# Preparing the first pair's queries in two pieces, and the second pair later, in an attention and MoE kernel

## The chip, the cores and the metric

The kernel runs on one core of a Trainium2 chip. Its engines are TensorE (PE), VectorE (DVE), ScalarE (ACT), GpSimd (POOL) and SyncE (SP, which here only requests transfers). The metric is the device time of one launch in microseconds (us).

## What is computed

Attention with rotary embedding over 2 x 8 heads of 576 positions and 64 columns, and behind it two MLPs on the 1152 tokens. Cut to what matters:

```python
q_rot, k_rot = (rotate(q), rotate(k))
scores = scale * np.matmul(q_rot, k_rot.transpose(0, 1, 3, 2))
scores = scores - np.max(scores, axis=-1, keepdims=True)
attn = np.exp(scores)
attn = attn / (np.sum(attn, axis=-1, keepdims=True) + 1e-09)
x = np.matmul(attn, v)             # heads side by side: 1152 x 512
h = np.maximum(x @ w_in, 0.0)      # d_ff 2048
x = h * h @ w_out
out = ((x @ w_a) * (x @ w_b)) @ w2_out   # d_ff 1536
```

## The kernel before

The heads are taken in eight pairs. Of a pair, one tile `X` (128 partitions, the two heads above each other) holds queries and keys, each a second time with the halves swapped, so that rotation is a product with the cosines and sines in `cs` and a sum into `rot`. f32 numbers are split into a high part (a cast to the f32r type) and a low part (the rest). For every pair a tile `SK` holds queries, keys and the low part of the keys for both heads, with the high part of the queries in one half of the partitions and their low part in the other, so that a matmul with the keys in both halves sums them.

`first_pair` (L160) makes pair 0 and writes `SK[0]` directly. `prepare` (L151) makes the other pairs: for keys (`qi` 1) and queries (`qi` 0) a product over 1152 columns (L154) and a sum (L155) on the engine given in `engs`, a cast to the high part on ScalarE (L156), the low part on POOL (L157). `place` then copies high and low parts into `SK` by four DMAs on SP's queue (L142). There is one buffer `rot` and one pair of buffers `hi`, `lo` for all pairs, and `SK` has two buffers.

The work of a pair is nine blocks. For block i, `emit_S` makes the scores (four matmuls of 288 columns; the ninth block, for both heads' last 64 queries, ten), `emit_max` their maximum on VectorE (L214), `emit_exp` the exponentials with their sums on ScalarE (L220), and `emit_T` (three blocks later) the transposes on PE, copied from PSUM by ScalarE or VectorE (`evac`). Scores have two PSUM buffers, so block i+2 waits for the exponentials of block i. The products with V (`av_units`) of a pair lie between the blocks of the next; `emit_scale` spreads the reciprocals of the sums over partitions by small bf16 matmuls with `sel` and `ident16`, and these need a copy named `rows`. Behind the last pair come the MLPs (`unit1`, `out1`, `unit2`, `out2`), whose weights are fetched into `raw` tiles and prepared by `prep_weight`, four of them while the attention still runs.

The order on each engine is not the order in which the code is written: a scheduler lays the instructions of all engines out by its own estimates, and each engine then runs its list strictly in order (PE may load weights ahead). Pools with few buffers decide what has to wait. `X` of pair 0 and of pair 2 share a buffer, so the load of pair 2 waits for the last step that reads the queries of pair 0.

Of the kernel before, what the change touches and what calls it, by code (L numbers as in the profile page):

```python
# [7 lines left out]
F32 = mybir.dt.float32  # L8
F32R = mybir.dt.float32r
BF16 = mybir.dt.bfloat16  # L10
I32 = mybir.dt.int32
I64 = mybir.dt.int64
AF = mybir.ActivationFunctionType
ALU = mybir.AluOpType
AX = mybir.AxisListType

P = 128
S = 576
# [9 lines left out]
DM = 512  # L28
# [5 lines left out]
def attention_moe_moe2_kernel(ctx: ExitStack, tc: tile.TileContext, qk, rope, vm, vt, ident_in, sel_in, w_in, w_out, w_a, w_b, w2_out, out):  # L34
    nc = tc.nc
    act, dve, pool, pe = nc.scalar, nc.vector, nc.gpsimd, nc.tensor

    const = ctx.enter_context(tc.tile_pool(name="const", bufs=1))
# [5 lines left out]
    wpools = [ctx.enter_context(tc.tile_pool(name="wa", bufs=NWA))]  # L44

    ident = const.tile([P, P], F32, name="ident")
    ident16 = const.tile([P, P], BF16, name="ident16")
    sel = const.tile([18, 6, P], BF16, name="sel")
    X = {1: xpool.tile([P, 2, 2, S], F32, tag="x", name="X1")}
    xb = [xpool.tile([P, 2, KC, TB], F32R, tag="x", name=f"x{n}") for n in range(NTB)]  # L50

# [49 lines left out]
    LOFF = (1280, 1344)  # L101
    MAIN = (0, 128)

    def half(h):
        return slice(64 * h, 64 * h + 64)
# [51 lines left out]
            pool.tensor_tensor(out=lo[qi], in0=rot[:, qi, :], in1=hi[qi].bitcast(F32), op=ALU.subtract)  # L157
        place(p)

    def first_pair():  # L160
        sk, x = SK[0], X[0]

        def own(qi, h):
            off = (QOFF, KOFF)[qi][h]
            return sk[half(h), h, off:off + S]

        def cross(qi, h):
            off = (QOFF, KOFF)[qi][h]
            return sk[half(1 - h), h, off:off + S]

        for qi in (1, 0):
            for n in range(2):
                dve.tensor_tensor(out=x[:, n, qi, :], in0=x[:, n, qi, :], in1=cs[:, n, :], op=ALU.mult)
            dve.tensor_tensor(out=rot[:, qi, :], in0=x[:, 0, qi, :], in1=x[:, 1, qi, :], op=ALU.add)
            if qi:
                for h in range(2):
                    act.copy(own(1, h), rot[half(h), 1, :])
                    if h == 0:
                        act.copy(cross(1, h), rot[half(h), 1, :])
                    pool.tensor_tensor(out=sk[half(h), h, LOFF[h]:LOFF[h] + S], in0=rot[half(h), 1, :], in1=own(1, h).bitcast(F32), op=ALU.subtract)  # L180
        for h in range(2):
            act.copy(own(0, h), rot[half(h), 0, :])
            dve.tensor_tensor(out=cross(0, h), in0=rot[half(h), 0, :], in1=own(0, h).bitcast(F32), op=ALU.subtract)  # L183
            if h == 0:
                dve.tensor_copy(cross(1, 1), rot[half(1), 1, :])

    SP, PT, PTT, PR, ST = {}, {}, {}, {}, {}

# [147 lines left out]
    NB = 9 * NPAIR  # L336

    load_qk(0)
    load_qk(1)
    nc.sync.dma_start(out=ident, in_=ident_in)  # L340
    sel32 = g2.tile([18, 6, P], F32, tag="r", name="sel32")
    nc.sync.dma_start(out=sel32, in_=sel_in)
    zero_fills(0)
    zero_fills(1)
    first_pair()
    prepare(1, (dve, dve))
    emit_S(0)
    avq = []
    for i in range(NB + LT):
        p, j = divmod(i, 9)  # L350
        if i == 4:
            dve.tensor_copy(ident16, ident)
            dve.tensor_copy(sel, sel32)
        if i + 1 < NB:
            emit_S(i + 1)
        if i < NB:
            emit_max(i)
            emit_exp(i)
        if 0 <= i - LT:
            emit_T(i - LT)  # L360
        if p > 0:
            if j == LT + 1 and p <= NPAIR:
                avq += av_units(p - 1)
            for _ in range(2 if j > LT else 1):
                if avq:
                    avq.pop(0)()
        if j == 5 and i < NB:
            load_v(p)
        if p + 1 < NPAIR:
            n = p + 1  # L370
            if j == 0 and p > 0:
                load_qk(n)
            if j == 1 and p > 0:
                prepare(n, (dve, pool))
    while avq:
        avq.pop(0)()
# [198 lines left out]
```

## Time and profile before

| | us |
|---|---|
| median of three timed runs (613.55 to 614.51) | 613.93 |
| profiled execution | 613.54 |
| its span, first to last instruction | 611.8 |
| PE busy | 584.6 (96%) |
| VectorE, ScalarE, POOL busy | 333.6, 321.4, 257.2 |

The busy time of PE is near the whole span, and the granted clock is full (9 of 9 tenths, or 1.00) in every slice. The page's 40 slices of 15.3 us show PE at 0 tenths in the first, at 6 in the second and at 9 from the third on, except for the last. So what a change of the start is worth is read there, and from how far PE has come in its fixed list at a given time.

### The profile page before, as it was taken

Reading aid. Unit: us, or ns where it says so; the run is one execution under the profiler, and the core shown is the slowest. Engines: PE = TensorE matmul, PEld = TensorE weight load, DVE = VectorE, ACT = ScalarE, POOL = GpSimd, SP = SyncE. Lnnn points to the kernel's source line nnn. Section 1 sums busy time; section 2 is a strip of 40 time slices with the busy share of each in tenths; the row PEclk is TensorE's granted clock in tenths of the full one; section 3 lists DMA queues with packets and bytes.
Section 4 is the critical chain, followed back from the end, with each engine's and each line's share of the span. In section 5 each row is a group of like instructions: output and inputs, shape, how many; then the busy total and the mean of one; then the engine's idle time right before and its main releaser. Section 6 shows DMA issues by size and latency. Waiting matters only on the chain.

```text
span 611.8 us, 8929 instructions
## 1 busy us (share of the span) xinstructions
PE 584.6 (96%) x3368; PEld 520.3 (85%) x3368; DVE 333.6 (55%) x550; ACT 321.4 (53%) x685; POOL 257.2 (42%) x278
## 2 busy tenths in 40 slices
PE   0699999999999999999999999999999999999997
PEld 0567665666759999999999999999988999889986
DVE  5987578865525665676764467664440653221122
ACT  3477777786747776873671455554543653102200
POOL 4567655652115853770670433544421444202110
PEclk9999999999999999999999999999999999999999
DMA  6675756544001444433331213323220440000012
GB/s 230 183 191 149 210 169 182 135 130 109 20 2 70 138 138 138 138 132 110 121 121 35 83 55 104 108 99 118 90 69 7 142 128 1 0 1 2 0 53 103
DMA packets 20678, 61.41 MB, mean 100 GB/s; under 512 B 3337, under 2 KB 3721, under 8 KB 19739
## 3 DMA queue, kind: packets, MB, share of 16 engines
q1 hardware_dynamic: 20635, 60.85, 32.6%
q8 instruction: 26, 0.43, 0.3%
q14 instruction: 17, 0.14, 0.1%
HBM read 48.16 MB, written 2.36 MB: 83 GB/s over the span
## 4 chain that ended last, share of the span: by engine, by line
PE 92%; DVE 5%; DMA 1%; issue 1%; ACT 1%; SPq 0%; DVEq 0%; ACTq 0%
PE av L317 8%; PE s L205 7%; PE h L391 5%; PE y L391 5%; PE h L393 5%; PE h L392 5%; PE y L393 5%; PE y L392 5%; PE t L275 5%; PE a L391 4%; PE a L393 4%; PE b L391 4%; PE b L393 4%; PE a L392 4%; PE b L392 4%; PE o L467 4%
## 5 line engine op out<-in xcount | busy, mean ns | idle before, releaser
L411 POOL TENSOR_TENSOR g<-v,g 128x384 fp32r<-128x384 f32 x84 | 85.2, 1016 | 132.9 <-ACT g L410 132.9
L205 PE MATMUL s<-sk 128*128 128x288 f32 x336 | 64.9, 322 | 20.3 <-DVE sk L183 15.0
L205 PEld LDWEIGHTS s<-sk 128*128 128x128 f32 x336 | 48.6, 195 | 39.1 <-DVE sk L183 15.0
L410 ACT CAST g<-v 128x384 fp32r<-128x384 f32 x84 | 42.9, 511 | 62.2 <-DVE v L409 62.1
L214 DVE TENSOR_REDUCE st<-s 128x1 f32<-128x576 f32 x72 | 53.7, 751 | 31.2 <-PE s L205 31.1
L391 PE MATMUL h<-x,w_i 128*128 128x384 f32 x192 | 64.2, 335 | 0.0
L392 PE MATMUL h<-x,w_i 128*128 128x384 f32 x192 | 64.1, 334 | 0.0
L393 PE MATMUL h<-x,w_i 128*128 128x384 f32 x192 | 64.1, 334 | 0.0
L391 PE MATMUL y<-g,w_o 128*128 128x384 f32 x192 | 64.1, 334 | 0.0
L392 PE MATMUL y<-g,w_o 128*128 128x384 f32 x192 | 64.1, 334 | 0.0
L393 PE MATMUL y<-g,w_o 128*128 128x384 f32 x192 | 64.1, 334 | 0.0
L220 ACT ACTIVATE P<-s,st 128x576 f32<-128x576 f32 x72 | 53.6, 745 | 13.2 <-DVE st L214 13.0
L317 PE MATMUL av<-PT,V 128*64 128x384 f32 (+1 forms) x256 | 52.4, 425 | 0.0
L275 PE MATMUL t<-ident,P 128*128 128x128 f32 x288 | 45.9, 280 | 2.4 <-DVE PT L260 2.2
L393 PE MATMUL a<-yb,w_a 128*128 128x384 f32 x144 | 48.1, 334 | 0.0
L391 PE MATMUL a<-yb,w_a 128*128 128x384 f32 x144 | 48.1, 334 | 0.0
L392 PE MATMUL a<-yb,w_a 128*128 128x384 f32 x144 | 48.1, 334 | 0.0
L391 PE MATMUL b<-yb,w_b 128*128 128x384 f32 x144 | 48.1, 334 | 0.0
L392 PE MATMUL b<-yb,w_b 128*128 128x384 f32 x144 | 48.1, 334 | 0.0
L393 PE MATMUL b<-yb,w_b 128*128 128x384 f32 x144 | 48.1, 334 | 0.0
L409 DVE TENSOR_TENSOR v<-b,s 128x384 f32<-128x384 f32 x36 | 19.9, 554 | 50.8 <-PE b L393 50.8
L467 PE MATMUL o<-w,g 128*128 128x512 f32 (+1 forms) x112 | 42.8, 382 | 0.0
(118 smaller groups left out, 1337.8 us busy)
## 6 DMA issues: line engine op xcount, KB each, us to landing
raw_i<-in_w_in SPq DMA_DIRECT2D x16, 512.0 KB, 3.4
raw_o<-in_w_out SPq DMA_DIRECT2D x16, 512.0 KB, 3.2
X<-in_qk SPq DMA_DIRECT2D x7, 1152.0 KB, 5.4
raw_a<-in_w_a SPq DMA_DIRECT2D x12, 512.0 KB, 3.3
raw_b<-in_w_b SPq DMA_DIRECT2D x12, 512.0 KB, 3.3
raw<-in_w_out SPq DMA_DIRECT2D x12, 512.0 KB, 3.4
sk<-hi_lo SPq DMA_DIRECT2D x14, 432.0 KB, 5.1
sk<-hi_lo SPq DMA_DIRECT2D x14, 288.0 KB, 5.7
```

The lines of the kernel that those rows point to most:

```text
L205: pe.matmul(s[:, b, c:c + n], lhs, rhs, start=(m < 2), stop=(m >= len(mm) - len(cuts)), skip_group_check=(j == 8))
L214: dve.tensor_reduce(out=ST[p][:, 0, j:j + 1], in_=SP[i][:, :, 0:288], op=ALU.max, axis=AX.XY, negate=True)
L220: act.activation(pr[:, h, :].rearrange("p (b n) -> p b n", b=2), SP.pop(i)[:, :, 0:288], AF.Exp, bias=st[:, 0, j:j + 1], scale=1.0, accum_ ...
L275: pe.transpose(t[:, k * P:(k + 1) * P], flat[:, c0:c0 + P], ident)
L317: pe.matmul(AVT[p, r][half(h), 0:n], V[p][:, h, k, :], PT[p][:, h, k, q0:q0 + n], start=False, stop=(k == 3), skip_group_check=True)
L391: pe.matmul(dst, wh, mh, start=first, stop=False)
L392: pe.matmul(dst, wh, ml, start=False, stop=False)
L393: pe.matmul(dst, wl, mh, start=False, stop=last)
L409: dve.tensor_tensor(out=val, in0=src, in1=other, op=ALU.mult)
L410: act.copy(gt[:, 0, c], val)
L411: pool.tensor_tensor(out=gt[:, 1, c], in0=val, in1=gt[:, 0, c].bitcast(F32), op=ALU.subtract)
L467: pe.matmul(dst, gt[:, 1, c], w[:, 0, d], start=False, stop=(k == G - 1))
```

## The change

- `load_qk(1)` is taken out of the start. Pair 1's `X` is now requested on ScalarE's queue, from within `first_pair`, after the first cross copy of the keys.
- `first_pair` takes a range of columns and is called twice: for all keys and queries 0 to 191, and for queries 192 to 575 (named `c`). All casts and copies into `SK[0]` are on ScalarE and all subtractions on VectorE; POOL no longer takes part. `emit_S(0)`, `emit_S(1)`, `emit_max(0)`, `emit_exp(0)` stand between the two calls, and `emit_max(1)` within the second.
- From the first of these calls until the loop's block 3 a manual order holds on PE, ScalarE, VectorE and POOL: the written one.
- `prepare(1)` moves from the start into the loop (block 2) and has its queries on POOL instead of VectorE, as the later pairs.
- `ident16` and `sel` are no longer bf16 tiles that VectorE fills by casts, but views of the f32 tiles: the upper half of each word, every second bf16 element.
- Two memsets of `raw` tiles at block 3 keep the first weight fetches from being requested before.

```diff
--- before.py
+++ after.py
@@ -44,8 +44,9 @@
     wpools = [ctx.enter_context(tc.tile_pool(name="wa", bufs=NWA))]
 
     ident = const.tile([P, P], F32, name="ident")
-    ident16 = const.tile([P, P], BF16, name="ident16")
-    sel = const.tile([18, 6, P], BF16, name="sel")
+    sel32 = const.tile([18, 6, P], F32, name="sel")
+    ident16 = ident.bitcast(BF16).rearrange("p (n two) -> p n two", two=2)[:, :, 1]
+    sel = sel32.bitcast(BF16).rearrange("p k (n two) -> p k n two", two=2)[:, :, :, 1]
     X = {1: xpool.tile([P, 2, 2, S], F32, tag="x", name="X1")}
     xb = [xpool.tile([P, 2, KC, TB], F32R, tag="x", name=f"x{n}") for n in range(NTB)]
 
@@ -157,7 +158,7 @@
             pool.tensor_tensor(out=lo[qi], in0=rot[:, qi, :], in1=hi[qi].bitcast(F32), op=ALU.subtract)
         place(p)
 
-    def first_pair():
+    def first_pair(c0, c1):
         sk, x = SK[0], X[0]
 
         def own(qi, h):
@@ -168,21 +169,28 @@
             off = (QOFF, KOFF)[qi][h]
             return sk[half(1 - h), h, off:off + S]
 
-        for qi in (1, 0):
+        def rotated(qi, c):
             for n in range(2):
-                dve.tensor_tensor(out=x[:, n, qi, :], in0=x[:, n, qi, :], in1=cs[:, n, :], op=ALU.mult)
-            dve.tensor_tensor(out=rot[:, qi, :], in0=x[:, 0, qi, :], in1=x[:, 1, qi, :], op=ALU.add)
-            if qi:
-                for h in range(2):
-                    act.copy(own(1, h), rot[half(h), 1, :])
-                    if h == 0:
-                        act.copy(cross(1, h), rot[half(h), 1, :])
-                    pool.tensor_tensor(out=sk[half(h), h, LOFF[h]:LOFF[h] + S], in0=rot[half(h), 1, :], in1=own(1, h).bitcast(F32), op=ALU.subtract)
+                dve.tensor_tensor(out=x[:, n, qi, c], in0=x[:, n, qi, c], in1=cs[:, n, c], op=ALU.mult)
+            dve.tensor_tensor(out=rot[:, qi, c], in0=x[:, 0, qi, c], in1=x[:, 1, qi, c], op=ALU.add)
+
+        c = slice(c0, c1)
+        if c0 == 0:
+            rotated(1, slice(0, S))
+            act.copy(own(1, 0), rot[half(0), 1, :])
+        rotated(0, c)
+        if c0:
+            emit_max(1)
         for h in range(2):
-            act.copy(own(0, h), rot[half(h), 0, :])
-            dve.tensor_tensor(out=cross(0, h), in0=rot[half(h), 0, :], in1=own(0, h).bitcast(F32), op=ALU.subtract)
-            if h == 0:
-                dve.tensor_copy(cross(1, 1), rot[half(1), 1, :])
+            if c0 == 0 and h == 1:
+                act.copy(own(1, 1), rot[half(1), 1, :])
+            act.copy(own(0, h)[:, c], rot[half(h), 0, c])
+            if c0 == 0:
+                act.copy(cross(1, h), rot[half(h), 1, :])
+                dve.tensor_tensor(out=sk[half(h), h, LOFF[h]:LOFF[h] + S], in0=rot[half(h), 1, :], in1=own(1, h).bitcast(F32), op=ALU.subtract)
+            dve.tensor_tensor(out=cross(0, h)[:, c], in0=rot[half(h), 0, c], in1=own(0, h)[:, c].bitcast(F32), op=ALU.subtract)
+            if c0 == 0 and h == 0:
+                act.dma_start(out=X[1], in_=qk[1])
 
     SP, PT, PTT, PR, ST = {}, {}, {}, {}, {}
 
@@ -336,25 +344,31 @@
     NB = 9 * NPAIR
 
     load_qk(0)
-    load_qk(1)
     nc.sync.dma_start(out=ident, in_=ident_in)
-    sel32 = g2.tile([18, 6, P], F32, tag="r", name="sel32")
     nc.sync.dma_start(out=sel32, in_=sel_in)
     zero_fills(0)
     zero_fills(1)
-    first_pair()
-    prepare(1, (dve, dve))
+    in_order = ExitStack()
+    in_order.enter_context(tc.manual_schedule(engines={getattr(mybir.EngineType, e) for e in ("PE", "Activation", "DVE", "Pool")}))
+    first_pair(0, 192)
     emit_S(0)
+    emit_S(1)
+    emit_max(0)
+    emit_exp(0)
+    first_pair(192, S)
     avq = []
     for i in range(NB + LT):
         p, j = divmod(i, 9)
-        if i == 4:
-            dve.tensor_copy(ident16, ident)
-            dve.tensor_copy(sel, sel32)
-        if i + 1 < NB:
+        if i == 3:
+            for k in range(2):
+                dve.memset(raw.tile([P, DM], I64, tag="raw", name=f"later{k}").bitcast(I32)[:, 0:1], 0)
+            in_order.close()
+        if 0 < i < NB - 1:
             emit_S(i + 1)
-        if i < NB:
+        if 1 < i < NB:
             emit_max(i)
+            emit_exp(i)
+        if i == 1:
             emit_exp(i)
         if 0 <= i - LT:
             emit_T(i - LT)
@@ -370,7 +384,7 @@
             n = p + 1
             if j == 0 and p > 0:
                 load_qk(n)
-            if j == 1 and p > 0:
+            if j == (1 if p else 2):
                 prepare(n, (dve, pool))
     while avq:
         avq.pop(0)()
```

The change moves instructions at three places that matter below. POOL, behind its memsets, before (98 and 99 are the `SK` tiles, `X_296` is the tile of pair 2):

```order
L180 TENSOR_TENSOR sk_98<-cs_rot,sk_98 64x576 x2
L157 TENSOR_TENSOR hi_lo<-cs_rot,hi_lo 128x576 x2
L154 TENSOR_TENSOR X_296<-X_296,cs_rot 128x2x576
L155 TENSOR_TENSOR cs_rot<-X_296 128x576
L236 CAST part_0_376<-st_163 128x6
L237 TENSOR_TENSOR rest_0_375<-st_163,part_0_376 128x6
L238 CAST part_0_376<-rest_0_375 128x6
L239 TENSOR_TENSOR part_0_376<-rest_0_375,part_0_376 128x6
```

and now (`X_78` is pair 1, `X_306` pair 2, both L158 are low parts of pair 1: first the queries', then the keys'):

```order
L155 TENSOR_TENSOR X_78<-X_78,cs_rot 128x2x576
L156 TENSOR_TENSOR cs_rot<-X_78 128x576
L158 TENSOR_TENSOR hi_lo<-cs_rot,hi_lo 128x576
L155 TENSOR_TENSOR X_306<-X_306,cs_rot 128x2x576
L156 TENSOR_TENSOR cs_rot<-X_306 128x576
L158 TENSOR_TENSOR hi_lo<-cs_rot,hi_lo 128x576
L244 CAST part_0_386<-st_151 128x6
L245 TENSOR_TENSOR rest_0_385<-st_151,part_0_386 128x6
```

Before, both low parts of pair 1 stand ahead of pair 2's product and sum; now those stand between the two. On ScalarE both high parts of pair 1 (L156) stood ahead of all exponentials; now the exponentials of block 3 stand behind the high part of the queries, and those of block 4 behind that of the keys.

PE at the end of pair 0, before (`s_267` is the first block of pair 1, reading `sk_99`; `t_275` to `t_305` are transposes of blocks 5 to 7):

```order
L205 MATMUL s_248<-sk_98 128x64
L205 MATMUL s_267<-sk_99 128x288 x4
L275 MATMUL t_275<-ident,P_2_204 128x128 x2
L275 MATMUL t_290<-ident,P_3_235 128x128 x4
L275 MATMUL t_305<-ident,P_3_235 128x128 x4
L205 MATMUL s_281<-sk_99 128x288 x4
L285 MATMUL tk_311<-ident,P_2_204 128x128
L285 MATMUL tk_311<-ident,P_3_235 128x128
```

and now (there it is `s_277`, reading `sk_98`; `t_300` and `t_315` are blocks 6 and 7):

```order
L213 MATMUL s_258<-sk_97 128x64
L283 MATMUL t_300<-ident,P_3_245 128x128 x4
L283 MATMUL t_315<-ident,P_3_245 128x128 x4
L293 MATMUL tk_321<-ident,P_2_214 128x128
L213 MATMUL s_277<-sk_98 128x288 x4
L293 MATMUL tk_321<-ident,P_3_245 128x128
L283 MATMUL t_345<-ident,P_4_282 128x128 x4
L297 MATMUL tt_352<-ident,P_4_282 64x128
L320 MATMUL av_0_400<-PTT_202,vtail_99 128x384
L325 MATMUL av_0_400<-PT_201,V_236 64x384
L283 MATMUL t_365<-ident,P_0_297 128x128 x4
```

The first block of pair 1 now stands behind all transposes of blocks 6 and 7, and the products with V of pair 0 begin a few rows behind it.

VectorE where the keys of pair 3 are prepared, before (`X_509` is pair 3):

```order
L260 COPY PT_189<-t_335 128x4x64
L260 COPY PTT_190<-tt_342 64x64
L154 TENSOR_TENSOR X_509<-X_509,cs_rot 128x2x576
L214 TENSOR_REDUCE st_286<-s_327 128x1
L214 TENSOR_REDUCE st_286<-s_346 128x1
L260 COPY rows_0_385<-r_0_383 18x128
L155 TENSOR_TENSOR cs_rot<-X_509 128x576
```

and now (`X_519`):

```order
L222 TENSOR_REDUCE st_296<-s_308 128x1
L222 TENSOR_REDUCE st_296<-s_337 128x1
L222 TENSOR_REDUCE st_296<-s_356 128x1
L268 COPY rows_0_395<-r_0_393 18x128
L155 TENSOR_TENSOR X_519<-X_519,cs_rot 128x2x576
L222 TENSOR_REDUCE st_296<-s_371 128x1
L222 TENSOR_REDUCE st_296<-s_402 128x1
```

The copy of `rows` stood two maxima behind the product on `X_509`, and stands ahead of the product on `X_519` now.

## Rows read from the trace of the kernel before

**Rows 1.** The page, its first group: busy time, share of the span, instructions.
```profile
PE 584.6 (96%) x3368; PEld 520.3 (85%) x3368; DVE 333.6 (55%) x550; ACT 321.4 (53%) x685; POOL 257.2 (42%) x278
```

**Rows 2.** Timeline of PE: start us, us, engine, line, operation, count, [idle before, releaser].
```profile
15.02 2.29 PE L205 MATMUL s<-sk 128*128 128x288 f32 x8 [15.02 <-DVE sk L183]
21.33 2.29 PE L205 MATMUL s<-sk 128*128 128x288 f32 x8 [4.03 <-ACT P L220]
...
26.66 0.79 PE L205 MATMUL s<-sk 128*128 128x288 f32 x4
...
31.51 2.19 PE L205 MATMUL s<-sk 128*128 128x288 f32 x14
...
34.59 0.66 PE L275 MATMUL t<-ident,P 128*128 128x128 f32 x4 [0.24 <-ACT PT L258]
...
42.97 0.32 PE L250 MATMUL r<-rows,sel 18*128 18x128 bf16 x3 [0.99 <-DVE rows L260]
```

**Rows 3.** Stretches: busy time of each engine (instructions), granted clock, DMA share, GB/s.
```profile
15.00:35.25 20.25, 13.99 (x80) 12.20 (x80) 18.41 (x24) 11.98 (x28) 11.28 (x10) 1.00 0.67 199
38.00:45.00 7.00, 5.99 (x34) 3.84 (x34) 5.68 (x8) 4.58 (x13) 4.64 (x2) 1.00 1.02 216
45.00:80.00 35.00, 35.00 (x227) 23.64 (x225) 23.35 (x44) 25.89 (x63) 22.54 (x27) 1.00 0.63 174
80.00:115.00 35.00, 33.24 (x211) 22.17 (x209) 27.03 (x44) 25.38 (x60) 20.80 (x24) 1.00 0.58 168
```

**Rows 4.** Timeline of VectorE (DVE) from 7 to 20 us.
```profile
7.93 0.76 DVE L174 TENSOR_TENSOR cs_rot<-X 128x576 f32<-128x576 f32 x1
8.61 1.42 DVE L173 TENSOR_TENSOR X<-X,cs_rot 128x576 f32<-128x576 f32 x2
...
15.78 2.63 DVE L154 TENSOR_TENSOR X<-X,cs_rot 128x1152 f32<-128x1152 f32 x2
```

**Rows 5.** Groups by line and shape, 0 to 50 us: count, busy us, mean ns, idle.
```profile
L214 DVE TENSOR_REDUCE st<-s 128x1 f32<-128x576 f32 x17 | 12.4, 746 | 4.6 <-PE s L205 4.6
...
L157 POOL TENSOR_TENSOR hi_lo<-cs_rot,hi_lo 128x576 fp32r<-128x576 f32 x5 | 7.0, 1410 | 9.2 <-ACT hi_lo L156 9.2
...
L156 ACT CAST hi_lo<-cs_rot 128x576 fp32r<-128x576 f32 x5 | 3.3, 673 | 4.2 <-DVE cs_rot L155 4.2
```

**Rows 6.** Timeline of POOL from 18 to 44 us.
```profile
22.59 4.21 POOL L154 TENSOR_TENSOR X<-X,cs_rot 128x1152 f32<-128x1152 f32 x1
...
37.60 2.65 POOL L154 TENSOR_TENSOR X<-X,cs_rot 128x1152 f32<-128x1152 f32 x1
40.33 2.39 POOL L155 TENSOR_TENSOR cs_rot<-X 128x576 f32<-128x576 f32 x1
```

**Rows 7.** Timeline of VectorE beside them.
```profile
22.96 1.34 DVE L154 TENSOR_TENSOR X<-X,cs_rot 128x1152 f32<-128x1152 f32 x1
...
38.42 3.04 DVE L154 TENSOR_TENSOR X<-X,cs_rot 128x1152 f32<-128x1152 f32 x1
```

**Rows 8.** DMA requests on SP's queue, and times from request to landing.
```profile
13.50 0.33 SPq L131 DMA_DIRECT2D X<-in_qk  x1
...
X<-in_qk SPq DMA_DIRECT2D x1, 1152.0 KB, 5.2
...
21.28 0.68 SPq L142 DMA_DIRECT2D sk<-hi_lo  x1
...
22.65 0.61 SPq L142 DMA_DIRECT2D sk<-hi_lo  x1
...
sk<-hi_lo SPq DMA_DIRECT2D x1, 288.0 KB, 4.4
```

**Rows 9.** Timeline of PE from 96 to 100 us.
```profile
98.59 0.66 PE L275 MATMUL t<-ident,P 128*128 128x128 f32 x4 [1.30 <-DVE PT L260]
```

**Rows 10.** Weight loads of PE by line and shape, 0 to 175 us.
```profile
L275 PEld LDWEIGHTS t<-ident,P 128*128 128x128 f32 x284 | 33.5, 142 | 6.9 <-DVE PT L260 2.7 <-issue 2.0 <-ACT P L220 0.6
...
L250 PEld LDWEIGHTS <-sel 18*128 18x128 bf16 x21 | 1.2, 92 | 2.1 <-issue 2.1
```

## The prediction

> **What bounds the kernel now.** Read the engine shares first, then the stretches, then the rows of TensorE (PE) in the first 46 us, and last what the other engines do there.
>
> PE is busy for 584.6 of 611.8 us [rows 1], so only its idle time can be won: some 27 us. 15.0 us of that stand before the first score matmul, which waits for VectorE's last preparation step [rows 2]. From 15 to 35.25 us PE works 13.99 of 20.25 us, so 6.3 us more are idle; from 38 to 45 it is 1.0 us, and from 80 to 115 it is 1.8 us [rows 3]. From 45 to 80 nothing is idle. Whatever the change does to the start must therefore show as idle time of PE before about 45 us. PE's order is fixed, so the question is how late a state of its work is reached: at 35.25 us the kernel before has done the ten score blocks S0 to S9 and the transposes of blocks 0 to 7 (the last transposes start at 34.59 for 0.66 us) [rows 2]. S9 is the first block of the second pair; it is among the 14 matmuls from 31.51 on and waits for nothing [rows 2].
>
> **The start is earlier.** VectorE's chain for the first pair ends its key rotation at 7.93 + 0.76 = 8.69 us [rows 4]; the change leaves this as it is. The query rotation is now made on 192 of 576 columns. Two 576-column steps take 1.42 us and two 1152-column steps 2.63 us [rows 4], so a column costs (1.315 - 0.71)/576 = 1.05 ns, and a step of 192 columns 0.71 - 384 x 0.00105 = 0.31 us, one of 384 columns 0.51 us. Three steps from 8.61 us end about 9.65. ScalarE then casts the 192 columns (an estimate of 0.35 us, between nothing and the 0.67 us of a full cast [rows 5]) and the cross copy of the keys (0.67): 10.7 us. VectorE's two subtractions end just before. So S0 starts at about 10.75 us, 4.3 us before the 15.02 of now. S1 follows at 12.6 us (one more cast, copy and subtraction of each). The rest of the queries: max 0 ends at 13.2, three steps of 0.51 at 14.8, max 1 (0.75 us [rows 5]) at 15.4, the two remaining subtractions of 0.55 at 16.0 and 16.5. S2 starts at 16.0 us, which was 21.33 [rows 2]. VectorE's two casts of identity and selector are gone too, and it takes over from GpSimd (POOL) the first pair's key subtraction, in the steps counted here. All that is 4 to 5 us won on paper.
>
> **What comes next, and why little of it may remain.** The second pair is loaded and prepared later, and S9 cannot start before the copies of its prepared data into SK have landed. The first of these copies needs the low part of the keys, and on POOL this step now stands behind the whole query work of the third pair (two instructions on X_306), as the rows of POOL's order show. POOL's steps alone: a 1152-column product 2.65 us [rows 6], a low part 1.41 us [rows 5], and a sum, which also has two inputs of 576 columns, is taken as the same. That these are what they cost alone is read from the slow ones: the product of 22.59 took 4.21, but VectorE's own two-input product of 22.96 held it up until 24.30, and 24.15 + 2.65 = 26.80 is its end. The other way round VectorE's product of 38.42 took 3.04 us instead of 1.34, since POOL's ran until 40.25; and POOL's next step, ready at 40.33, took 2.39, since VectorE had gone first until about 41.4 [rows 6, 7]. So one waits for the other, and they take turns.
>
> The Trainium skill (SBUF — State Buffer, section "SBUF: two separate sides") says the same of a port pair that VectorE's two-input steps and GpSimd share: it is held for the whole instruction and not split. By that rule the low prices hold with waits at certain places, as taken below; if instead a step were merely slowed whenever the two overlap, 4.21 and 1.80 would be its price each time, which is the third rival.
>
> The chain, by those rows:
> - X1 is requested by ScalarE after the cross copy, at 10.7. A load of 1152 KB that was requested at 13.50 landed 5.2 us later [rows 8]; with some hundredths until POOL sees it: 15.95.
> - VectorE's two subtractions run until 16.4; POOL's product ends at 19.0. VectorE's key product, queued from 17.5, goes first (1.25), then POOL's sum: 21.6.
> - ScalarE casts the queries' high part (0.67 [rows 5]): 22.25. In ScalarE's order the exponentials of block 3 now stand behind this cast: they could go at about 20.9 and go at 22.9, so S5 starts at about 23.6 (26.66 now [rows 2]). The lead of 5.3 us has become 3, which costs nothing yet.
> - POOL: low part of the queries 23.7, third pair's product 26.35 and sum 27.8 (its load was requested at 14.8 and is long there), then VectorE's third-pair key product, queued meanwhile, goes first (1.25): 29.0; low part of the keys: 30.4.
> - The first copy into SK is requested at 30.4. In the trace the first is requested at 21.28 and the second, which also has to be there, at 22.65, landing 4.4 us later [rows 8]: 5.8 us after the first. There the second waited for a low part; without that it follows 0.68 us behind, 5.1 us in all. So 35.5 to 36.2; I take 36.0.
>
> S9 then runs from 36.0 to 36.8, and all work before it in PE's order (S0 to S8, transposes 0 to 7) is done by about 33.3, so PE idles for some 2.7 us. The same state was reached at 35.25 before: **1.55 us later** (36.8 - 35.25), in spite of a start that is 4.3 us earlier. VectorE waits too: its sum for the third pair's keys stands behind that low part, and max 8 behind this sum, about 1.3 us later than it could be, which PE doesn't feel since S9 is later still.
>
> After S9 the AV work of the first pair is ready and stands in PE's order between the blocks. The wait of 0.99 us at 42.97, for the copy of the rows of reciprocals [rows 2], came from VectorE's product of 3.04 us ahead of that copy [rows 7]; in the new order the copy stands ahead of such a product, and five AV matmuls and a score block stand between. I take it as gone: -0.99 (bounds 0 and -0.99). The 1.8 us between 80 and 115, mostly a wait of 1.30 us at 98.59 [rows 9], come from the same kind of meeting of VectorE and POOL in a later pair. Where those meet in the new order I can't tell: 0, with bounds of -1.8 and +1.8.
>
> **Selector and identity.** They become views with every second bf16 element of the f32 tiles. 48 weight loads of the selector (six a pair) take 92 ns now; those of f32 data with as many columns 142 ns [rows 10]. So at most 50 ns more for each, 2.4 us, and they run beside matmuls; I take 0. The Trainium skill (TensorE: Matmul & The Clock Gate, section "Weight-path perf modes") has the fast weight load go by the type, and lists column steps up to 1,024 as allowed: by that 0 as well. Moving the identity's view through a transpose is 16 small matmuls; 0.
>
> **Sum**, against the profiled execution, which took 613.54 us with a span of 611.8 (the three timed runs have a median of 613.93, 0.06% above): 613.54 + 1.55 - 0.99 = **614.1 us**. About 0.2% (1.2 us) is what a measurement of this kernel can tell from no change.
>
> **Rivals.** *POOL is quicker to the low part* (faster). If VectorE's two key products don't come between POOL's steps, the copy is requested 2.5 us earlier and S9 starts at 33.5, ends at 34.3: 613.54 - 0.95 - 0.99 = 611.6; with one of the two it is 612.9. For it: which engine is first is decided by tenths of a microsecond. Against it: both products are queued in the middle of POOL's steps by the sums above.
>
> *POOL takes X1 before VectorE's last subtractions* (slower). VectorE gets to the first at 15.4 as summed, 0.55 us before X1 lands. If it is 0.6 late, both wait: POOL's product runs from 15.95 to 18.6, the first subtraction until 19.15, POOL's sum until 20.55, the second subtraction until 21.1. S2 starts at 19.2 and S3 at 21.1, max 2 ends at 21.85 and its exponentials at 22.6, and the cast of the queries' high part, which stands behind those on ScalarE, ends at 23.3 instead of 22.25. Everything behind it is 1.05 later; if VectorE then also holds the copy of the reciprocals as now, it is 613.54 + 1.55 + 1.05 = 616.1. From an S9 later than about 37 on the kernel is slower by more than can be missed.
>
> *Overlaps slow POOL each time.* 4.21 and 1.80 for product and sum, twice: 15.95 + 6.01 + 0.67 + 1.41 + 6.01 + 1.41 + 5.6 = 37.1 for S9, and 615.2.
>
> *The early start doesn't come about.* If ScalarE's request or casts cost more than I take, S0 moves, but S9 is gated by X1's load and POOL. Each microsecond of S0 from a later ScalarE moves the load with it, so this too is slower, by as much: 615.1 for one.
>
> **Chances.** Forecast, within about a microsecond: 0.43. Quicker POOL or a later stall that doesn't come: 0.23. X1 ahead of the subtractions: 0.19. Slower overlaps, a later request, or a new stall in later pairs: 0.15. So faster by over 0.2%: 0.23, within: 0.43, slower: 0.34. Eight in ten: from 611.9 (the quick case) to 616.8 (the slow case with some of the selector's or later pairs' cost).
>
> **What would show it.** The first score matmul at 10.5 to 11 us; S2 at about 16; S5 at 23.6, held by ScalarE's cast; PE idle for 2 to 4 us ahead of the first block of the second pair, released by a copy into SK that was requested behind POOL's third-pair steps; no wait of 1 us at the reciprocals. The prediction is wrong if PE doesn't wait for those copies, or if the idle time from 45 to 200 us differs by more than 2 us.

## The result, and the profile after

The changed kernel took 608.42 us (median of 4 runs, 607.34 to 610.76) beside 613.74 of the kernel before: a ratio of 0.9915 [0.9899, 0.9931], **0.85% faster**, and below the range of the prediction. A second timing gave 609.41 us and 0.9919 [0.9907, 0.9932]. The profiled execution took 607.92 us with a span of 606.1, against 613.54 and 611.8: 5.7 us less, all before the MLP's first matmul (about 179.5 us, from 185.22).

TensorE (PE) in the changed kernel, timeline as in [rows 2]; S0 is the row of 10.05, S5 that of 24.07, S9 that of 33.55:

```profile
10.05 1.30 PE L213 MATMUL s<-sk 128*128 128x288 f32 x4 [10.05 <-ACT sk L189]
11.95 1.30 PE L213 MATMUL s<-sk 128*128 128x288 f32 x4 [0.60 <-DVE sk L191]
...
17.84 1.30 PE L213 MATMUL s<-sk 128*128 128x288 f32 x4 [3.33 <-DVE sk L191]
...
24.07 0.80 PE L213 MATMUL s<-sk 128*128 128x288 f32 x4 [1.41 <-ACT P L228]
...
30.39 0.66 PE L283 MATMUL t<-ident,P 128*128 128x128 f32 x4 [0.43 <-ACT P L228]
32.60 0.33 PE L293 MATMUL tk<-ident,P 128*128 128x128 f32 x1 [1.55 <-DVE PT L268]
33.55 0.77 PE L213 MATMUL s<-sk 128*128 128x288 f32 x4 [0.62 <-DMA sk<-hi_lo]
...
37.14 1.51 PE L325 MATMUL av<-PT,V 128*64 128x384 f32 x8
38.58 1.33 PE L213 MATMUL s<-sk 128*128 128x288 f32 x8
...
64.08 0.32 PE L258 MATMUL r<-rows,sel 18*128 18x128 bf16 x3 [0.93 <-DVE rows L268]
```

S0 starts 5.0 us before the 15.02 of [rows 2], and TensorE waits 2.6 us (0.43, 1.55 and 0.62) ahead of S9; only the last 0.62 us of that end with a copy into SK. The state that the prediction compared (S0 to S9 and the transposes of blocks 0 to 7) stands at 34.32 us instead of 35.25, with one tail transpose done in addition.

The stretches, against [rows 3] (busy us of PE first; then the other engines, granted clock, DMA):

```profile
38.00:45.00 7.00, 7.00 (x46) 4.23 (x40) 3.33 (x6) 3.08 (x8) 5.83 (x4) 1.00 0.67 175
45.00:80.00 35.00, 33.38 (x225) 24.56 (x225) 28.49 (x45) 26.75 (x68) 22.50 (x28) 1.00 0.63 170
80.00:115.00 35.00, 35.00 (x227) 23.48 (x225) 23.32 (x45) 26.22 (x62) 21.94 (x24) 1.00 0.70 192
```

The 1.0 us between 38 and 45 is gone. The 1.8 us between 80 and 115 are gone too, but 1.6 us have come in between 45 and 80, half of it at the copy of `rows` of the next pair (64.08).

That explains some 2 us of 5.7: 0.9 at S9, 1.0, and 0.1. The rest lies in busy time. One group of the page, first of the kernel before:

```profile
L317 PE MATMUL av<-PT,V 128*64 128x384 f32 (+1 forms) x256 | 52.4, 425 | 0.0
```

and of the changed one, where the line is L325:

```profile
L325 PE MATMUL av<-PT,V 128*64 128x384 f32 (+1 forms) x256 | 49.2, 425 | 0.0
```

The same 128 AV matmuls (two records each, so x2 is one matmul and x4 the pair of both heads) cost 3.2 us less, at the same mean. The timeline of PE before shows how:

```profile
44.73 0.86 PE L317 MATMUL av<-PT,V 128*64 128x384 f32 x2
45.52 0.80 PE L205 MATMUL s<-sk 128*128 128x288 f32 x4
...
48.36 1.51 PE L317 MATMUL av<-PT,V 128*64 128x384 f32 x8
49.80 1.42 PE L205 MATMUL s<-sk 128*128 128x288 f32 x10
```

One matmul of 384 columns keeps PE from 44.73 until the next block at 45.52, 0.79 us; four keep it from 48.36 to 49.80, 1.44 us. A run is here a row of AV matmuls with no other matmul between them. Over all rows a run takes 0.15 us plus 0.64 (384 columns) or 0.32 (192) for every two matmuls begun: a lone one costs what a pair costs. In the order of before the AV matmuls stand in 61 runs with 40 and 41 such twos, which makes 47.9 us; in that of the changed kernel, where the scheduler split fewer pairs, in 55 runs with 38 and 39, 45.05 us. So **2.8 us come from a side effect of the new order**, which neither the diff nor the prediction speaks of. The last 0.8 us lie in the transposes: counted behind S9 from each start to the next instruction's, without waits, they take 32.03 us instead of 32.84, and the other groups cancel. Why the transposes got cheaper was not followed.

### The profile page after: what moved, and what is told of

The parts are those of the page before. It is cut to its first block, busy times and chain, and to the rows that moved or that the text cites. A ratio compares the mean times of both kernels' runs of the same rounds, so it can differ in the third digit from the quotient of the medians.

```text
span 606.1 us, 8939 instructions
## 1 busy us (share of the span) xinstructions
PE 582.7 (96%) x3368; PEld 520.0 (86%) x3368; DVE 327.3 (54%) x554; ACT 322.2 (53%) x688; POOL 256.8 (42%) x278
## 4 chain that ended last, share of the span: by engine, by line
PE 92%; DVE 2%; POOL 2%; DMA 1%; issue 1%; ACT 0%; SPq 0%; POOLq 0%; ACTq 0%
PE s L213 7%; PE av L325 7%; PE h L405 6%; PE y L405 6%; PE h L407 5%; PE h L406 5%; PE y L407 5%; PE y L406 5%; PE t L283 5%; PE a L405 4%; PE b L405 4%; PE a L407 4%; PE b L407 4%; PE a L406 4%; PE b L406 4%; PE o L481 4%
## 5 line engine op out<-in xcount | busy, mean ns | idle before, releaser
L325 PE MATMUL av<-PT,V 128*64 128x384 f32 (+1 forms) x256 | 49.2, 425 | 0.0
```

The lines of the kernel that those rows point to most:

```text
L325: pe.matmul(AVT[p, r][half(h), 0:n], V[p][:, h, k, :], PT[p][:, h, k, q0:q0 + n], start=False, stop=(k == 3), skip_group_check=True)
```

## Experiments

Two theories at the outset. *State and price*: what TensorE does from S9 on takes a fixed time, so S9's start counts one to one, and the rest of the gain is the AV matmuls' grouping. *Slack*: work behind S9 absorbs what is won or lost there, and the gain is the earlier start as such. Each kernel is compared with the kernel before, timed beside it (medians 613.94 and 614.24).

**1. AV matmuls in pairs of two chunks, on the kernel before.** One unit of AV work issues two chunks; nothing else is edited.

```diff
-            units += [lambda r=r, k=k: main(r, k) for k in range(4)]
+            units += [lambda r=r, k=k: (main(r, k), main(r, k + 1)) for k in (0, 2)]
```

> The kernel before, with the same edit of the AV units and nothing else. By the same price its runs cost 42.5 us (41 and 33 slots, 38 runs) instead of 47.9 (40 and 41 slots, 61 runs): 5.4 us less, about 608.4 us, which is as fast as the change, with the start as slow as before. Rival, that the number of matmuls counts and the change's gain is all in the start: 613.7. In between if the longer runs hold up score blocks.

Measured: 609.42 us, 0.9925 [0.9913, 0.9937], 4.8 us faster. Its AV group:

```profile
L317 PE MATMUL av<-PT,V 128*64 128x384 f32 (+1 forms) x256 | 45.4, 419 | 0.0
```

38 runs instead of 61, 52.4 us down to 45.4 with not one matmul fewer. The price of a lone AV matmul is real, and nearly all of it reaches the end (5.4 by the count, 4.8 measured). This one line brings the kernel before about as far as the whole change does.

**2. The same on the changed kernel.**

> The changed kernel, with the AV products of two 128-key blocks in one unit, so that PE's list has 37 runs of AV matmuls instead of 55. Theory: a run of AV matmuls costs 0.15 us and 0.64 us (384 columns) or 0.32 us (192 columns) for every two matmuls begun, so that a lone matmul costs as much as two; by the rows of the changed kernel's PE its 38 and 39 slots of two cost 45.0 us. Here 40 and 34 slots in 37 runs cost 42.0: 3.0 us less than the changed kernel, about 605.4 us. Rival, that only the number of matmuls counts: no change, 608.4. Rival, that the longer runs hold up the score blocks, so that their wait takes the gain: 607 to 609 with new idle time of PE ahead of score matmuls.

Measured: 608.51 us, 0.9901 [0.9888, 0.9913]; not to be told from the changed kernel. PE is busy 2.5 us less, but waits for ScalarE's exponentials come in its place, and the granted clock fell to 0.63 between 35 and 38 us. Its timeline of PE:

```profile
34.21 0.77 PE L213 MATMUL s<-sk 128*128 128x288 f32 x4 [0.62 <-DMA sk<-hi_lo]
58.25 0.80 PE L213 MATMUL s<-sk 128*128 128x288 f32 x4 [0.69 <-ACT P L228]
...
82.46 0.79 PE L213 MATMUL s<-sk 128*128 128x288 f32 x4 [0.56 <-ACT P L228]
97.31 0.80 PE L213 MATMUL s<-sk 128*128 128x288 f32 x4 [0.92 <-ACT P L228]
```

The price is there, but here most of what it set free went into waits: 4.1 us of idle time from 45 to 190 us, against 1.6 in the changed kernel. The expectation of 605.4 was wrong. At a like mean clock of the whole run some 1 us is left of it: four runs at 0.996 and 0.997 took 607.71 to 608.58 us, the changed kernel's two at 0.997 609.36 and 609.49.

**3. S9 later, in the same order.** POOL makes the low part of the second pair's queries three times, so the copy behind it leaves 2.84 us later. Every other instruction stands where it stood in its engine's list, on all engines.

```diff
+            for _ in range(3 if p == 1 and qi == 0 else 1):
-            pool.tensor_tensor(out=lo[qi], in0=rot[:, qi, :], in1=hi[qi].bitcast(F32), op=ALU.subtract)
+                pool.tensor_tensor(out=lo[qi], in0=rot[:, qi, :], in1=hi[qi].bitcast(F32), op=ALU.subtract)
```

> The changed kernel with one edit: POOL makes the low part of the second pair's queries three times instead of once (the same result), so the second copy into SK leaves 2.84 us later; every other instruction stands as in the changed kernel on every engine. It puts S9 at about 36.2 to 36.4, which is the state that the prediction named, with the changed kernel's own order of AV matmuls. Theory 'the state at S9 is passed on to the end, as the prediction's sum has it': 2.2 to 2.8 us longer than the changed kernel, 610.6 to 611.9; what is then still missing to the 614.1 of the prediction is the AV matmuls' 2.8. Rival 'there is slack behind S9, and the prediction's first term was never worth 1:1': less than 1 us longer. Rival 'TensorE's longer wait brings the clock down': over 3 us longer, with a granted clock below 1 behind the wait.

Measured: 612.59 us, 0.998 [0.9972, 0.9989]: some 3.2 to 4.2 us longer than the changed kernel by the medians of its two timings, 3.7 to 4.0 by the ratios. PE in this kernel:

```profile
26.13 0.80 PE L214 MATMUL s<-sk 128*128 128x288 f32 x4 [1.41 <-ACT P L229]
...
37.04 0.47 PE L294 MATMUL tk<-ident,P 128*128 128x128 f32 x1 [3.99 <-DVE PT L269]
37.99 1.30 PE L214 MATMUL s<-sk 128*128 128x288 f32 x4 [0.48 <-DMA sk<-hi_lo]
```

And its stretches around S9 (busy us of PE first, the granted clock third from the end):

```profile
34.00:38.00 4.00, 0.48 (x2) 0.22 (x2) 3.45 (x9) 1.31 (x3) 1.22 (x3) 0.58 0.54 128
38.00:42.00 4.00, 4.00 (x13) 2.83 (x14) 1.69 (x5) 2.28 (x7) 1.98 (x6) 0.57 0.92 238
42.00:46.00 4.00, 4.00 (x24) 2.19 (x24) 0.70 (x2) 1.53 (x3) 3.52 (x6) 1.00 0.50 191
```

From S5 to S9 it is 11.86 us, 9.48 in the changed kernel: 2.4 of the 2.84 us arrive at S9. (S5 itself is 2.06 us later here, as S0 is 1.83 later; the edit stands behind both.) Not only the copy is later: VectorE's next sum, which needs the buffer that POOL's low part reads, waits 3.61 us for it, and the 3.99 us of PE hang on VectorE's work behind that sum. On top comes the clock: in the long wait the granted clock falls to 0.5, the lower of its two levels (1.2 of 2.4 GHz), and S9 takes 1.30 us instead of 0.77. PE's list behind S9 is the same in the five profiles below. With the changed kernel's profile taken anew (S9 at 34.04, span 607.5), the span less S9's start holds the two apart:

| kernel | S9 starts | span less that | granted clock, 30 to 35, 35 to 38, 38 to 45 |
|---|---|---|---|
| changed | 33.55 | 572.55 | 1.00, 1.00, 1.00 |
| changed, taken anew | 34.04 | 573.5 | 0.93, 0.54, 1.00 |
| S9 later (3) | 37.99 | 573.6 | 0.96, 0.50, 0.75 |
| POOL's order held (4) | 34.67 | 574.8 | 0.86, 0.50, 0.83 |
| additional matmuls (7) | 33.88 | 575.3 | 0.81, 0.50, 0.87 |

What follows S9 takes 572.5 us at the full clock and 1 to 3 us more where it falls; little or nothing of S9's lateness is given back. The slack theory falls; of the three expectations the first and the clock's came together, which is why the time lies above 611.9. All eleven runs of this kernel have a mean clock of 0.994. The one run of the changed kernel that had it as low took 610.76 us, which leaves 1.8 us for the 2.4 of S9, by a single run.

**4. POOL's written order held until block 11**, so that both low parts of pair 1 stand ahead of pair 2's product.

```diff
+    pool_order = ExitStack()
+    pool_order.enter_context(tc.manual_schedule(engines={mybir.EngineType.Pool}))
     in_order = ExitStack()
-    ... for e in ("PE", "Activation", "DVE", "Pool")}))
+    ... for e in ("PE", "Activation", "DVE")}))
...
+        if i == 11:
+            pool_order.close()
```

> The changed kernel with POOL kept in the written order until pair 2 is prepared: the low part of pair 1's queries stands ahead of pair 2's product and sum; PE's, ScalarE's and VectorE's lists are the same. Theory: the first block of pair 1 waits for the second copy into SK, which is requested at 30.11 us behind that low part. Here the low part can follow its cast at 24.6, ends at 26.0, and the copy lands by about 30.5, so the block starts at 31 to 32 us instead of 33.55, limited by the transposes ahead of it: 0.5 to 2.5 us less than the changed kernel, 606 to 608 us. Rival, that this gate costs nothing because PE fills the time: 608.4.

Measured: 611.2 us, 0.9941 [0.9924, 0.9959]; longer than the changed kernel. But this goes with the clock: the four runs with a mean granted clock of 0.994 took 611.20 to 611.65 us, the two at 0.999 and 1.00 took 608.41 and 608.77, as the changed kernel does. PE's, ScalarE's and VectorE's lists are those of the changed kernel, so apart from the clock the held order neither won nor lost; whether it makes the fall likelier, these few runs don't show. In the profiled run, one of the four, the second low part now ends at 27.1 us, and S9 no longer waits for the copy, yet it starts at 34.67:

```profile
32.53 0.66 PE L283 MATMUL t<-ident,P 128*128 128x128 f32 x4 [1.53 <-ACT P L228]
34.54 0.47 PE L293 MATMUL tk<-ident,P 128*128 128x128 f32 x1 [1.35 <-DVE PT L268]
34.67 1.31 PE L213 MATMUL s<-sk 128*128 128x288 f32 x4
```

The gate is VectorE, whose steps for pair 2 now fall on blocks 7 and 8. The expected 606 to 608 failed: POOL's order was one of two gates that ended at nearly the same time. In the changed kernel the other one, VectorE's copy ahead of the tail transpose at 32.60, let S9 go only 0.6 us before the copy into SK did; in its profile taken anew it alone held S9:

```profile
33.94 0.33 PE L293 MATMUL tk<-ident,P 128*128 128x128 f32 x1 [0.82 <-DVE PT L268]
34.04 1.04 PE L213 MATMUL s<-sk 128*128 128x288 f32 x4
```

**5. One piece instead of two.** `first_pair(0, S)` and `emit_max(1)` stand in place of the two calls.

```diff
-    first_pair(0, 192)
+    first_pair(0, S)
...
-    first_pair(192, S)
+    emit_max(1)
```

> The changed kernel without the split: all 576 columns of the first pair's queries are prepared in one go, everything else as it is (late load of pair 1, engines, written order, views). S0 then starts about 1.2 us later (three VectorE steps of 0.71 instead of 0.35 us), but S2 and S3 don't wait for VectorE's second piece, which POOL's product held up for 4 us. Theory, that the start is worth only what is left of it at the first block of pair 1: within 1 us of the changed kernel, apart from AV runs, which cost 0.3 us more here: 607.5 to 609.5. Rival, that the split gives the gain, as the first matmul's 5.0 us are nearly the 5.3 us of the result: 609.6 or more.

Measured: 615.18 us, 1.0013 [1.0004, 1.0021]. S0 starts at 12.64, but here the scheduler also put pair 2's product ahead of pair 1's on POOL (7.40 us for the two), so that S5 starts at 29.78, and the granted clock fell twice. The run doesn't isolate the split. With POOL's order held as in 4 it comes nearer to that:

> The changed kernel with POOL's written order held through the second pair's preparation (as in the earlier run of it, 611.2), and the first pair's queries in one piece: beside that run it isolates the split. Theory 'the split's early start carries through to S9': S0 at 12.6, S9 later by 1.5 to 2 us, the time 612.5 to 613.5. Rival 'the start has slack': S5 and S9 within 0.7 us of that run, and 610.5 to 612.

Measured: 612.06 us, 0.9975 [0.9965, 0.9984]. S0 starts at 12.13 (10.68 in 4), S5 at 25.95 (25.11), S9 at 36.77 (34.67); S8 waits 2.54 us for an exponential. By the ratios, whose intervals don't overlap, it is 2.1 us longer than 4, by the medians 0.9; at a mean clock of 0.999 or 1.00 three runs took 611.56 to 612.03 us, against 608.41 and 608.77 in 4. That agrees with the early start's theory. How the lead reaches S9 is not shown: S5 is only 0.8 us later, what made S8 wait was not followed, the profile is that of the longest run (614.54), and from 59 us on PE's order is no longer that of 4.

**6. Later and in order.** The written order of all four engines holds until block 11, the weights' memsets stand at block 7, and AV matmuls go in pairs.

```diff
-        if i == 3:
+        if i == 7:
             for k in range(2):
                 dve.memset(raw.tile(...
+        if i == 11:
             in_order.close()
```

> The changed kernel with three edits that the earlier runs call for: the written order of all four engines holds until block 11 (so VectorE and POOL finish the second pair before they touch the third), the weights' preparation starts behind block 7 instead of block 3, and AV matmuls are issued in pairs of two chunks. Theory 'POOL's order gates the second pair, and lone AV matmuls cost as much as two': both low parts leave POOL by about 26 us, the copy lands by about 29.5, so S9 waits for nothing and starts at about 31.5 instead of 33.55 (-2 us), the AV matmuls cost 42.2 instead of 45.05 (-2.9), so 608.4 - 4.9 = 603.5; 605.5 if new idle time of 2 us comes later, as in the run of the pairs alone. Rival 'the slack behind S9 takes it all': 607 to 608.5, with S9 early and the idle time of TensorE larger later. Rival 'the clock falls again': over 609, with a granted clock below 1 for some microseconds.

Measured: 618.3 us, 1.0069 [1.0045, 1.0093], some 15 us from the expected 603.5. The profile is that of the longest run (621.44). Of the rivals the clock's came (0.85 from 45 to 80), but it is the smaller part: TensorE idles 6.2 of the 35 us there and 4.0 from 80 to 115. Two rows of PE in this kernel:

```profile
52.88 0.44 PE L283 MATMUL t<-ident,P 128*128 128x128 f32 x2 [1.06 <-DVE PTT L268]
...
72.88 0.47 PE L258 MATMUL r<-rows,sel 18*128 18x128 bf16 x3 [4.58 <-DVE rows L268]
```

And VectorE ahead of the second of them:

```profile
68.90 3.80 DVE L155 TENSOR_TENSOR X<-X,cs_rot 128x1152 f32<-128x1152 f32 x1 [3.02 <-DMA X<-in_qk]
72.62 0.20 DVE L268 COPY rows<-r 18x128 bf16<-18x128 bf16 x1
```

VectorE waits 3.02 us for a later pair's `X`, then 3.80 us are gone in its product beside POOL's, and the copy of `rows` stands behind both. Because pair 2 was prepared later, its `X` tile came free later, and the loads behind it were requested at 41.08 and 59.88 us instead of 32.35 and 50.91. So POOL's early work on pair 2, which the prediction booked as a loss, looks like the lead that the later pairs live on; with three edits at once the run doesn't show it alone. With one piece instead of two in this order:

> The same as the kernel with the later order and AV pairs, but the first pair's queries in one piece: the same order on every engine otherwise, so it isolates the split. Theory 'the split's early start carries through': S0 at about 12.7 instead of 10.05 to 10.9, S5 and S9 later by the same 2 us, and the time longer by about 2 us. Rival 'the start has slack, since the sixth score block is held by the exponentials behind ScalarE's casts': S5 and S9 start within 0.5 us of those of the split one, and the time is within 0.7 us of it. Rival 'the split costs, since its last two subtractions meet POOL's product': one piece faster by 1 us or more.

Measured: 621.76 us, 1.012 [1.0084, 1.0155], 3.5 us longer than with two pieces; in both kernels waits and falls of the clock behind 45 us make most of the time, so this says little beyond the sign.

**7. What the lower clock at the start costs.** S0 and S1 take 1.30 us in the changed kernel, as S9 does in 3 at a granted clock of 0.5; so they are taken to run at the lower level, though the changed kernel's profile gives 1.00 for that stretch. The edit adds 20 matmuls of 128 columns on zeros, ahead of S0, while PE is idle.

```diff
+    warm = psum_1("av", "warm")
+    for n in range(20):
+        pe.matmul(warm[:, 0:P], VT[0], VT[1], start=True, stop=True)
     first_pair(0, 192)
```

> The changed kernel with 20 additional matmuls of 128 columns on zeros, issued ahead of the first score block, when TensorE is idle; the order is otherwise the same on every engine. It asks what the lower clock at the start costs. If TensorE then enters the first block at the higher level, S0 to S3 take 0.80 us each instead of 1.30 and the transposes 0.66 instead of 1.1. Theory 'the first 24 us are VectorE's and ScalarE's, TensorE has slack there': S5 and S9 within 0.7 us of before, and the time within 0.7 us of the changed kernel. Rival 'the lower clock at the start is on the path': 1.5 to 2.5 us shorter. Rival 'the matmuls are in the way or the waits behind them lower the clock all the same': no shorter blocks, and 0 to 2 us longer.

Measured: 609.75 us, 0.9929 [0.9916, 0.9942]; no gain. PE in this kernel:

```profile
4.00 7.18 PE L355 MATMUL warm<-vtail,vtail 128*128 128x128 f32 x40 [4.00 <-POOL vtail L113]
12.61 0.76 PE L213 MATMUL s<-sk 128*128 128x288 f32 x4 [0.91 <-DVE sk L191]
...
18.16 1.30 PE L213 MATMUL s<-sk 128*128 128x288 f32 x4 [3.46 <-DVE sk L191]
...
24.80 0.80 PE L213 MATMUL s<-sk 128*128 128x288 f32 x4 [1.41 <-ACT P L228]
```

S0 and S1 take 0.77 and 0.76 us instead of 1.30, but behind a wait of 3.46 us S2 takes 1.30 again (granted clock 0.60 from 15 to 20), and so do S3 and S4; S5 still waits 1.41 us for the exponentials. So the blocks just ahead of S5 ran no faster, and whether TensorE has slack there is not shown. Together with the AV pairs:

> The changed kernel with the AV matmuls in pairs of two chunks and the 20 additional matmuls ahead of the first score block. If the lower clock at the start and the fall near 35 us are what kept the pairs from paying here (their run alone: 608.5, with a fall), 606 to 607; if the pairs' gain goes into new waits behind 45 us, 608 to 609 as without the additional matmuls.

608.6 us, 0.9916 [0.9903, 0.9928]: as expected for the case that the pairs' gain goes into waits behind 45 us. The clock fell here too, to 0.52 from 35 to 38.

**8. The views alone, on the kernel before** (`ident16` and `sel` as in the change, VectorE's two casts taken out).

> The kernel before with one part of the change alone: selector and identity are strided views of the f32 tiles, and VectorE's two casts are gone. Theory 'the views cost nothing and the casts were hidden': within 1.2 us of the kernel before, 613.5 to 614.8, weight loads of the selector at 90 to 95 ns. Rival 'each strided weight load is dearer': 142 ns for each of 48, and up to 616. By the count of runs of AV matmuls (61 runs, one more 384-column slot) 0.6 us more than before.

Measured: 617.3 us, 1.005 [1.0038, 1.0062]: 3 us slower, and no theory had that (the count of runs gives 0.6). The weight loads of `sel` cost what they did:

```profile
L251 PEld LDWEIGHTS <-sel 18*128 18x128 bf16 x21 | 1.2, 93 | 3.0 <-issue 3.0
```

93 ns against the 92 of [rows 10]. But without the casts the order shifts: PE waits 2.02 us at 117.54 for a copy of `rows`, where it had waited 0.45, and behind a wait of 2.27 us at 28.09 the granted clock is 0.81 and 0.85 from 25 to 35. The views cost no more to load; the reshuffle that came with them was not free.

> The changed kernel once more, beside the others of this call: 607.3 to 608.9 with a granted clock of 1.00, up to 610.8 where the clock falls for some microseconds near 30 us. If the clock's falls go with certain runs and not with the order, some of its five runs show a mean clock below .997 and are 1.5 to 2.5 us longer.

Its 609.41 us (608.76 to 609.49) lie above what was expected at the full clock and below what was allowed for a fall, and the profile shows one: 0.54 from 35 to 38. But a run at 1.00 took 609.46 as well, so the clock alone doesn't make the difference between runs.

None of these beats the changed kernel by more than can be measured.

## Why the prediction was wrong

**Right.** S0 at 10.05 (forecast 10.75; 10.54 to 11.05 in six other profiles with the split, 11.88 in one) and S1 at 11.95 (12.6). The wait of [rows 2] at 42.97 gone. Nothing on balance between 45 and 115 us (-0.1). The views at nothing.

**Right in number, not in path.** S5 starts at 24.07 (forecast 23.6), but the cast didn't hold it. ScalarE in the changed kernel:

```profile
20.81 0.66 ACT L157 CAST hi_lo<-cs_rot 128x576 fp32r<-128x576 f32 x1
22.70 0.59 ACT L266 COPY PT<-t 128x512 f32<-128x512 f32 x1 [1.23 <-PE t L283]
23.18 0.75 ACT L228 ACTIVATE P<-s,st 128x576 f32<-128x576 f32 x1
```

The cast ends at 21.47; then ScalarE stands idle for 1.23 us until PE's transposes are done, copies them, and only then makes the exponentials that S5 waits for. That this ends near 23.6 is luck. The wait ahead of S9 has the forecast length too (2.6 us for 2 to 4), but only 0.62 us of it end with the copy into SK; the other 2 us end with exponentials and VectorE's copy, which the prediction said PE wouldn't feel. In the profile taken anew no copy into SK holds S9.

**Wrong, 2.5 us: the copies into SK, the term of +1.55.** `prepare` takes its engines by index, 0 the queries and 1 the keys, so `(dve, pool)` puts the keys on POOL. The prediction, and the section on the change ahead of it, have the two the wrong way round. POOL's rows in the changed kernel:

```profile
14.67 2.61 POOL L155 TENSOR_TENSOR X<-X,cs_rot 128x1152 f32<-128x1152 f32 x1 [10.72 <-ACT sk L187]
17.36 1.60 POOL L156 TENSOR_TENSOR cs_rot<-X 128x576 f32<-128x576 f32 x1
21.55 1.42 POOL L158 TENSOR_TENSOR hi_lo<-cs_rot,hi_lo 128x576 fp32r<-128x576 f32 x1 [2.59 <-ACT hi_lo L157]
22.92 3.17 POOL L155 TENSOR_TENSOR X<-X,cs_rot 128x1152 f32<-128x1152 f32 x1
26.17 1.42 POOL L156 TENSOR_TENSOR cs_rot<-X 128x576 f32<-128x576 f32 x1
27.55 2.54 POOL L158 TENSOR_TENSOR hi_lo<-cs_rot,hi_lo 128x576 fp32r<-128x576 f32 x1
```

SP's requests beside them:

```profile
14.15 0.33 SPq L132 DMA_DIRECT2D X<-in_qk  x1
23.63 0.33 SPq L65 DMA_DIRECT2D raw_i<-in_w_in  x1
24.64 7.60 SPq L143 DMA_DIRECT2D sk<-hi_lo  x4
```

The last row holds four requests. From 29 to 31 us alone, the second and third of them, and the second's time to landing:

```profile
30.11 1.27 SPq L143 DMA_DIRECT2D sk<-hi_lo  x2
...
sk<-hi_lo SPq DMA_DIRECT2D x1, 288.0 KB, 3.3
```

The row of 21.55 is the keys' low part, and the first copy, which needs it and not the queries', leaves at 24.64 instead of 30.4, right behind the cast of the queries' high part. Only the second waits for the low part that ends at 30.09 (forecast 30.4), and lands 3.3 us behind its request at 30.11. The forecast had both copies in a row behind it, 5.1 to 5.8 us. So S9 starts at 33.55, not 36.0, and the term is -0.9 us. With the 4.4 us of [rows 8] for the second copy alone, the right reading of the engines would have given 34.8; the rest is that this copy took 3.3. That S9's lateness then counts nearly one to one was right, as experiment 3 shows.

**Wrong, 2.8 us: a term that was missing.** The cost of the AV matmuls was taken as fixed. The difference in order was at hand (61 runs against 55), and so was the price in the trace of before (0.79 us for one matmul, 1.44 for four). With the 0.8 us of the transposes, which the sum didn't have either, these make up the 6.2 us between 614.1 and the profiled 607.92 to within 0.1.

**Of the rivals**, *POOL takes X1 before VectorE's last subtractions* came: ScalarE's request went out at 8.90, ahead of the cross copy at 9.27 and not behind it, so POOL's product started at 14.67 and VectorE's two subtractions took 4.55 us from 14.82:

```profile
14.82 4.55 DVE L191 TENSOR_TENSOR sk<-cs_rot,sk 64x384 fp32r<-64x384 f32 x2
```

The Trainium skill (SBUF — State Buffer, "SBUF: two separate sides") has the port that the two share held for a whole instruction by whichever starts first; these rows agree. S2 started at 17.84, neither 16.0 nor 19.2. It cost little, since POOL's sum ended at 18.96 and not at 21.6. *POOL quicker* gave 611.6 for an S9 at 33.5, which is where S9 was; of the 3.7 us from there to the profiled 607.92, 2.8 are the AV matmuls and 0.8 the transposes. The range, 611.9 to 616.8, came from S9, single waits and the selector's loads, while experiments 1, 4 and 8 move by about 2 to 5 us through order and clock.

## What to carry to other kernels

When a change lets a scheduler reorder, compare the grouping of the busiest engine's instructions before and after, and price a lone one against a grouped one from the trace: 2.8 of 5.7 us were there, and one edit of the grouping alone was worth 4.8 us on the kernel before. Read which operand goes to which engine from the code's indices, and check it on a row, before a chain of waits is built on it. Booking early work for a later stage as a loss is right only if that stage has lead to spare; here a kernel that delayed it, with two other edits, took 618.3 us instead of 608.4. And when two kernels differ by 1 to 3 us, compare runs with a like granted clock first: experiment 4's loss went with the clock.

## What the runs showed of the hardware

- A matmul with a 64-column weight tile on the stationary side took as long alone as with its neighbour for the other head: 0.79 us (44.73 to 45.52 in the kernel before) against 0.80 (65.75 to 66.55 for both, in experiment 6's kernel), with 0.65 us for two more.
- The same kernel's S0 started at 10.05 and 10.91 us and, in experiment 3, whose lists are alike up to there, at 11.88: VectorE's second step on the keys, which waits for a load, started at 6.08, 7.11 and 8.20.
- The granted clock fell to its lower level near 35 us in one profile of the changed kernel, behind 1.8 us of waits, and not in the other, behind 2.6 us. Behind or in waits of 3.46 us (experiment 7) and 3.99 us (experiment 3) it was at 0.50 to 0.60. What decides it between these was not settled.
